# Load order and load sizes at the two ends of an attention decode step: wo in eight loads for four, w2 in four for one, K31 behind V29

## The chip, the cores and the metric

The kernel runs on one core of one Trainium2 chip. The metric is device time in microseconds (us) of one execution; the time before is 526.57 us, the median of 5 runs (525.69 to 527.09).

## The reference

A decode step for 4 sequences, one new token each, with D = 640, 32 heads of 192, a cache of 8,192 positions of which the last 2,048 are used (W = min(4096, max(256, 8192 // 4))), and a gated feed-forward of width F = 1,536. All inputs are bf16.

```python
xn  = layernorm(x)                                   # (4, 1, 640)
q   = (xn @ wq), 32 heads of 192
s   = einsum("bhqd,bhkd->bhqk", q, k_cache[:, :, -W:]) * 192 ** -0.5
o   = einsum("bhqk,bhkd->bhqd", softmax(s), v_cache[:, :, -W:])
out = x + o.reshape(4, 1, 6144) @ wo + (silu(xn @ w1) * (xn @ w3)) @ w2
```

Each head's used part of K, for all 4 sequences, is 3,072 KB, and so is its V. With wq, wo, w1, w3 and w2 the core reads 222.96 MB.

## The kernel before

*Loads.* All big loads are issued by SyncE (SP), in the order in which the program names them; SyncE waits at an issue until the buffer is free, and what stands behind it waits too. One K tile `kt` (L143) or V tile `vt` (L149) of a head is 128 rows of 24,576 B. There are 2 K buffers and 3 V buffers. At the start the three V buffers hold wq, in three transfers (L166); then come K0 and K1, and V0 as soon as the q matmuls have freed a buffer.

*Start.* x comes in through ScalarE's queue (L160), is normalised by VectorE and ScalarE (L195 to L212, result `xn`), and turned by TensorE into `xnT` (L217) and into the weights for w1, `xw`, `xh`, `xl` (L241 to L249). The rows of w1 are split: four rows on each of 128 partitions, then 64 rows as 128 half rows, and the last 64 rows as 60 and 4 "low" rows in a tile of their own, `w1e` (L409), whose unused partitions GpSimd sets to zero (L410). The low rows come in two transfers (L418: 12 rows of 15,360 B; L421: 12 rows of 1,024 B). `xm` and `xe` (L229 to L238) are copies of parts of xn laid out to match; GpSimd zeroes them first (L230, L234).

TensorE computes q on all partitions in two rounds of 30 matmuls (L263); six PSUM tiles a round are copied to `qbc`, three by VectorE and three by ScalarE in the first round, all by ScalarE in the second (L269, L271). VectorE then clears the accumulators (L277, L281), and the heads begin.

*A head.* It has four units (slots). VectorE multiplies a quarter of the K tile by q (`mult`, L298, 128x3072); TensorE adds groups of products with an identity (`adder`, L309); VectorE reduces the rest to scores (L317). A chain follows: the maximum (`lmax` L321, a transpose L326, `gmax` L331, `gneg` L334, back to all partitions L339, `negm` L342), the exponentials (L345), and `z` (L353), the exponentials laid out by sequence. TensorE multiplies z with V (`pv`, L361), ScalarE copies the result (`o_sb`, L364), and TensorE sums it over partitions into `po` (`ge_sum`, L382), with the sums of exponentials beside it (`ge_tot`, L369).

*Projection.* When a group of HG = 8 heads is in `po`, VectorE takes the reciprocal (L375), scales and transposes (`ge_turn`: og L387, oT L390), and TensorE multiplies by the group's 1,536 rows of wo and adds into `acc` (`ge_proj`, through L284). There are four groups; each takes one load of wo (128 rows of 15,360 B), save that the last one is cut into three (7, 3 and 2 twelfths of a row). There is one wo buffer, and w1e uses it first.

*Feed-forward.* w1 (L411, L412), w3 (L452) and w2 (L474) use one buffer after one another; w1's matmuls (`w1_in`, L428) run in slot 13, w3's in slot 23, and w2's (`ffn_out`, through L284) at the end.

*Order.* It is written out by hand: `add(slot, phase, fn, args)` puts each step into a table, and the steps are emitted by slot, then by phase, then in the order of the calls. K of head h is asked for at slot 4(h - 1), when the fourth multiply of head h - 2 frees its buffer, V at slot 4h + 2. At the end, K31 is asked for ahead of V29 (`early`) and goes into a V buffer; V31 goes into a K buffer. So the last loads are K30, K31, V29, V30, V31, w2 in one transfer, and the last group of wo in three. TensorE runs `ffn_out` (24 matmuls in pairs, one for each half of `acc`) and then the last `ge_proj` (24), and the result is cast by ScalarE and VectorE (L546, L547) and stored (L548).

Of the kernel before, what the change touches and what calls it, by code (L numbers as in the profile page):

```python
# [10 lines left out]
FP32 = mybir.dt.float32  # L11
# [53 lines left out]
def kernel(  # L65
# [12 lines left out]
    HG: int = 8,  # L78
    FG: int = 4,
# [23 lines left out]
    HB = HG * CT // P  # L103
    QW = HG * Dh
    RPP = QW // P
    RW = Dh // RPP
# [6 lines left out]
    assert (H * Dh) % QC == 0 and NQ % 6 == 0 and QW % P == 0 and Dh == RW * RPP and CT == HB * RW and P == FG * CT and F == FG * CT * FC  # L113
    assert 2 * H * Dh <= NJ * Dh and KBUFS == 2 and VBUFS == 3 and HB * (Dh + 1) <= 512 and H // HG > 1

# [8 lines left out]
    wopool = ctx.enter_context(tc.tile_pool(name="wo", bufs=1))  # L124
# [16 lines left out]
    def load_k(h):  # L141
        kt = (kpool if h < H - 1 else vpool).tile([P, NJ, Dh], BF16, tag="kt" if h < H - 1 else "vt", name="kt")
        nc.sync.dma_start(out=kt[:].rearrange("q j d -> q (j d)"),  # L143
                          in_=k_win[:, h].rearrange("b (p j) d -> p b (j d)", p=PB))
        kts[h] = kt

    def load_v(h):
        vt = (vpool if h < H - 1 else kpool).tile([P, NJ, Dh], BF16, tag="vt" if h < H - 1 else "kt", name="vt")
        nc.sync.dma_start(out=vt[:].rearrange("q j d -> q (j d)"),  # L149
                          in_=v_win[:, h].rearrange("b (p j) d -> p b (j d)", p=PB))  # L150
        vts[h] = vt

    def wo_load(hg, i0=0, i1=RPP):
        if i0 == 0:
            wos[hg] = wopool.tile([P, RPP * D], BF16, tag="wo", name="wo_t")
        nc.sync.dma_start(out=wos[hg][:, i0 * D:i1 * D],
                          in_=A_wo[hg * QW:(hg + 1) * QW, :].rearrange("(p i) n -> p i n", i=RPP)[:, i0:i1, :].rearrange("p i n -> p (i n)"))
# [66 lines left out]
    KM, LE, LI, LS = KC - 1, 3, 4, 5  # L224
    LP, LF = LE * LI, CT + LE * LI
    PH = D - KM * P - LP * LS - LI
    LB = KM * P + PH
    assert PH == P // 2 and F % LE == 0
    xm = ppool.tile([B, 2, PH, 2], BF16, tag="pr", name="xm")  # L229
    nc.gpsimd.memset(xm[:], 0.0)  # L230
    for i in range(2):
        nc.vector.tensor_copy(out=xm[:, i, :, i], in_=xn[:, KM * P:LB])
    xe = ppool.tile([B, LS + LE, LF], BF16, tag="pr", name="xe")
    nc.gpsimd.memset(xe[:], 0.0)  # L234
    nc.vector.tensor_copy(out=xe[:, 0:LS, CT:LF].rearrange("b s (e i) -> b s e i", i=LI),
                          in_=xn[:, LB:LB + LS * LP].rearrange("b (i e s) -> b s e i", e=LE, s=LS))
    for e in range(LE):
        nc.vector.tensor_copy(out=xe[:, LS + e, e * LI:(e + 1) * LI], in_=xn[:, LB + LS * LP:D])  # L238
    xw_ps = ps_t.tile([P, KM + 2 + LS + LE, B], BF16, tag="t", name="xw_ps")
# [4 lines left out]
    for i in range(LS + LE):  # L244
        nc.tensor.transpose(out=xw_ps[0:LF, KM + 2 + i, :], in_=xe[:, i, :], identity=idb[0:B, 0:B])

    def weights(name, p, c0, c1):
        t = const.tile([p, c1 - c0, NREP, B], BF16, name=name)
        nc.vector.tensor_copy(out=t[:], in_=xw_ps[0:p, c0:c1, :].unsqueeze(2).to_broadcast([p, c1 - c0, NREP, B]))  # L249
        return t  # L250

    xw = weights("xw", P, 0, KM)
    xh = weights("xh", P, KM, KM + 2)
    xl = weights("xl", LF, KM + 2, KM + 2 + LS + LE)
# [31 lines left out]
    def acc_add(lhsT, rhs, last=False):  # L286
        for i in range(2):
            acc_half(i, lhsT, rhs, last=last)

    po = ps_po.tile([P, HB * (Dh + 1)], FP32, name="po")  # L290
    po_v = po[:, 0:HB * Dh].rearrange("p (i x r) -> p i x r", x=HB, r=RW)
# [75 lines left out]
    def ge_tot(h):  # L367
        blk, x = (h % HG) // HB, h % HB
        nc.tensor.matmul(po[blk * CT:(blk + 1) * CT, HB * Dh + x:HB * Dh + x + 1], lhsT=tot_w[:].rearrange("p a b -> p (a b)"),  # L369
                         rhs=rsums.pop(h)[:], start=True, stop=True)  # L370
        chs.pop(h)

    def ge_rec(hg):
        rt = small.tile([P, HB], FP32, tag="rt", bufs=2, name="rt")
        nc.vector.reciprocal(out=rt[:], in_=po[:, HB * Dh:HB * (Dh + 1)])  # L375
        rts[hg] = rt

    def ge_sum(h):
        blk, x = (h % HG) // HB, h % HB
        o_sb = o_sbs.pop(h)  # L380
        for par in range(2):
            nc.tensor.matmul(po_v[blk * CT:(blk + 1) * CT, :, x, :], lhsT=sel_w[:, par].rearrange("p a b -> p (a b)"),  # L382
                             rhs=o_sb[:, par * Dh:(par + 1) * Dh].rearrange("p (r i) -> p i r", i=RPP), start=(par == 0), stop=(par == 1))

    def ge_turn(hg):
        og = small.tile([P, RPP, HB, RW], BF16, tag="og", bufs=1, name="og")
        nc.vector.tensor_tensor(out=og[:], in0=po_v, in1=rts.pop(hg)[:].unsqueeze(1).unsqueeze(3).to_broadcast([P, RPP, HB, RW]),  # L387
                                op=ALU.mult)
        oT = small.tile([P, RPP, CT], BF16, tag="oT", bufs=2, name="oT")
        nc.vector.transpose(out=oT[:].rearrange("p i r -> p (i r)"), in_=og[:].rearrange("p i x r -> p (i x r)"))  # L390
        oTs[hg] = oT

    def ge_proj(hg, i0, i1, last=False):
        oT, wo_t = oTs[hg], wos[hg]
        for i in range(i0, i1):
            acc_add(oT[:, i, 0:B], wo_t[:, i * D:(i + 1) * D], last=last and i == RPP - 1)

    FW = F // FG
# [5 lines left out]
    FM = KM * F  # L405

    def w1_load():
        wt = fpool.tile([P, FM + F // 2], BF16, tag="w", name="w1")
        we = wopool.tile([LF, LS, F], BF16, tag="wo", name="w1e")  # L409
        nc.gpsimd.memset(we[:], 0.0)  # L410
        nc.sync.dma_start(out=wt[:, 0:FM], in_=B_w1[0:KM * P, :].rearrange("(p kc) n -> p (kc n)", kc=KM))  # L411
        nc.sync.dma_start(out=wt[:, FM:], in_=B_w1[KM * P:LB, :].rearrange("r (h n) -> (r h) n", h=2))  # L412
        ffn["w1"], ffn["w1e"] = wt, we

    def w1_low(n):
        b0, we = LB + LS * LP, ffn["w1e"]
        if n == 0:
            nc.sync.dma_start(out=we[CT:LF].rearrange("p s n -> p (s n)"),  # L418
                              in_=B_w1[LB:b0, :].rearrange("(i e s) n -> e i (s n)", e=LE, s=LS))
        else:  # L420
            nc.sync.dma_start(out=we[0:LP, 0, 0:F // LE], in_=B_w1[b0:D, :].rearrange("i (e n) -> e i n", e=LE))  # L421

    def w1_in():
# [3 lines left out]
        def mm(w, lhsT, rhs, c0=0, start=False, stop=False):  # L427
            nc.tensor.matmul(ps[w * CT:(w + 1) * CT, c0:c0 + rhs.shape[1]], lhsT=lhsT.rearrange("p a b -> p (a b)"), rhs=rhs, start=start, stop=stop)  # L428

        def main(kc):  # L430
            for w in range(FG):
                mm(w, xw[:, kc], wt[:, kc * F + w * FW:kc * F + (w + 1) * FW], start=(kc == 0), stop=(kc == KM - 1))

        main(0)
        for w in range(FG):
            c0 = FM + (w % 2) * FW
            mm(w, xh[:, w // 2], wt[:, c0:c0 + FW])
        for i in range(LS):
            for w in range(FG):
                mm(w, xl[:, i], we[:, i, w * FW:(w + 1) * FW])  # L440
        FE = F // LE
        for e in range(LE):
            for w in range(FG):
                c0, c1 = max(e * FE, w * FW), min((e + 1) * FE, (w + 1) * FW)
                if c0 < c1:
                    mm(w, xl[:, LS + e], we[:, 0, c0 - e * FE:c1 - e * FE], c0 - w * FW)
# [8 lines left out]
    def w3_in():  # L455
        ffn["ps"] = ps_t.tile([P, FW], FP32, tag="t", name="f_ps")
        for kc in range(KC):
            for w in range(FG):
# [13 lines left out]
    def w2_load():  # L472
        wt = fpool.tile([P, FC, D], BF16, tag="w", name="w2")
        nc.sync.dma_start(out=wt[:].rearrange("p c n -> p (c n)"), in_=w2_v.rearrange("p c n -> p (c n)"))  # L474
        ffn["w2"] = wt

    def ffn_out():
        for c in range(FC):
            acc_add(hT[:, c, 0:B], ffn["w2"][:, c, :])
# [8 lines left out]

    ends = {H - 3: (NU - 1, NU), H - 2: (NU + 2, NU + 3), H - 1: (NU + 4, NU + 5)}
    early = {H - 1: (NU - 10, -1)}  # L490
    for h in range(H):
        u0, ul = h * GQ, h * GQ + GQ - 1
        if h >= KBUFS:
            add(*early.get(h, ((h - KBUFS + 1) * GQ, 0)), load_k, h)
# [20 lines left out]
    for hg in range(NG - 1):  # L515
        a = ((hg + 1) * HG - 1) * GQ + L + 3
        add(hg * HG * GQ + 17, 0, wo_load, hg)
        for n in range(4):
            add(a + n, 6, ge_proj, hg, n * RPP // 4, (n + 1) * RPP // 4)
    add(3, 0, w1_load)  # L520
    for n in range(2):
        add(5 + 3 * n, 1, w1_low, n)
# [9 lines left out]
    WOC = [0, RPP - 5, RPP - 2, RPP]  # L532
    for h in range(H - 2, H):
        add(NU - 6, 0, load_v, h)
    add(NU - 6, 0, w2_load)
    for i0, i1 in zip(WOC, WOC[1:]):
        add(NU - 6, 0, wo_load, NG - 1, i0, i1)
        add(e, 6, ge_proj, NG - 1, i0, i1, True)
    add(e - 1, 8, ffn_out)
# [39 lines left out]
```

## Time and profile before

| | |
|---|---|
| median of 5 runs | 526.57 us (525.69 to 527.09) |
| profiled execution: its time | 526.66 us |
| its span, first to last instruction | 524.8 us |
| granted TensorE clock, mean | 0.896 |
| TensorE, VectorE, ScalarE, GpSimd busy | 68%, 65%, 11%, 2% of the span |
| DMA queue of the loads, share of 16 engines | 99.1% |
| read from HBM | 222.96 MB, 425 GB/s over the span |

The page gives busy times, the span in 40 slices with the share of DMA time and GB/s, and groups of instructions with the idle time ahead of them and what ended it. From the trace one can ask for any stretch (busy time of each engine, clock, DMA share, GB/s), for the instructions in order of time, and for the packets of each transfer: a packet is one row of it, on one of the 16 DMA engines. A transfer has landed when the last of its engines has signalled it. An instruction's row reads: start, duration, engine, line, operation, tile written and tiles read, shapes, and in brackets the idle time ahead of it with what ended it.

### The profile page before, as it was taken

What the parts mean: (1) busy time and instruction counts of PE and PEld (TensorE: products, weight loads), DVE (VectorE), ACT (ScalarE), POOL (GpSimd) and SP (SyncE); (2) the same over time, 40 slices, a digit from 0 to 9 for tenths busy, and PEclk for the clock granted to TensorE, in tenths of its full rate; (3) what the DMA queues carried; (4) which work ended last, traced back from release to release, by engine and by line L of the source; (5) the groups of instructions that cost most, each with busy time, mean ns of one, the idle gap of its engine ahead of it and who ended that gap; (6) DMA issues with size and microseconds to landing.
All of it is one profiled execution on the core that took longest, in us unless ns stands there. A gap on an engine that the chain in (4) does not pass through costs nothing.

```text
span 524.8 us, 4807 instructions
## 1 busy us (share of the span) xinstructions
PE 357.5 (68%) x2347; PEld 76.1 (14%) x1652; DVE 340.2 (65%) x397; ACT 57.3 (11%) x179; POOL 8.2 (2%) x11
## 2 busy tenths in 40 slices
PE   0777877674668776683867776664776776675786
PEld 0100121111111111110111111111111121111122
DVE  3349776385666777673667867663776767666951
ACT  2030122000101110110110111100011110011010
POOL 4200000000000000000000000000000000000000
PEclk9988898876887998888797989988798898889998
DMA  9999999999999999999999999999999999999996
GB/s 388 425 442 393 434 430 422 432 436 433 435 428 435 430 429 432 433 433 433 430 433 428 431 434 433 428 435 431 435 427 439 425 431 438 427 436 427 438 423 267
DMA packets 11155, 223.27 MB, mean 425 GB/s; under 512 B 1246, under 2 KB 1394, under 8 KB 1650
## 3 DMA queue, kind: packets, MB, share of 16 engines
q1 hardware_dynamic: 11118, 222.96, 99.1%
q8 instruction: 16, 0.26, 0.2%
q14 instruction: 5, 0.04, 0.0%
q10 hardware_dynamic: 16, 0.01, 0.0%
HBM read 222.96 MB, written 0.01 MB: 425 GB/s over the span
## 4 chain that ended last, share of the span: by engine, by line
DMA 60%; DVE 19%; PE 16%; ACT 2%; issue 2%; SPq 0%; DVEq 0%
DMA kt<-in_A_k_cache_dram 52%; DVE pr L298 13%; PE ps L309 8%; DMA w<-in_B_w_dram 6%; PE po L382 3%; DVE sc L317 3%; PE qps L263 2%; DVE z L353 1%; DMA x_sb<-in_A_x_dram 1%; ACT ex L345 1%; PE acc L284 1%; DVE xn L212 1%; PE mt L339 1%; ACT L345 0%; PE f_ps L428 0%
## 5 line engine op out<-in xcount | busy, mean ns | idle before, releaser
L309 PE MATMUL ps<-pr,idb 128*128 128x512 bf16 x768 | 211.3, 416 | 142.5 <-DVE pr L298 142.5
L298 DVE TENSOR_TENSOR pr<-kt,qbc 128x3072 bf16<-128x3072 bf16 x128 | 223.5, 1747 | 100.9 <-DMA kt<-in_A_k_cache_dram 100.9
L317 DVE TENSOR_REDUCE sc<-ps 128x16 f32<-128x512 f32 x128 | 87.1, 681 | 2.4 <-PE ps L309 2.4
L361 PE MATMUL o_ps<-vt,z 128*8 128x384 bf16 x1024 | 56.0, 363 | 1.8 <-DMA vt<-in_A_v_cache_dram 1.8
L382 PE MATMUL po<-o_sb,sel_w 128*32 128x192 f32 x128 | 48.5, 513 | 1.1 <-ACT o_sb L364 1.1
L361 PEld LDWEIGHTS <-z 128*8 128x8 bf16 x1024 | 25.0, 92 | 100.7 <-issue 90.9
L353 DVE TENSOR_TENSOR z<-ex,mask_b 128x256 bf16<-128x256 bf16 x32 | 13.6, 425 | 36.1 <-ACT ex L345 36.0
L364 ACT COPY o_sb<-o_ps 128x384 f32<-128x384 f32 x32 | 15.3, 478 | 188.8 <-PE o_ps L361 188.8
L334 ACT ACTIVATE gneg<-gmax 1x128 f32<-1x128 f32 x32 | 9.8, 308 | 169.2 <-DVE gmax L331 169.2
L326 PEld LDWEIGHTS mt<-idf,lmax 128*1 128x1 f32 x32 | 3.3, 103 | 135.2 <-issue 133.2
L382 PEld LDWEIGHTS po<-o_sb,sel_w 128*32 128x32 f32 x128 | 14.1, 130 | 27.8 <-issue 24.4
L309 PEld LDWEIGHTS <-idb 128*128 128x128 bf16 x123 | 11.9, 97 | 37.5 <-issue 31.2
L339 PEld LDWEIGHTS mt<-ones_ff,gneg 1*128 1x128 f32 x64 | 9.4, 182 | 47.3 <-issue 40.0
L263 PE MATMUL qps<-wt,xnT 128*128 128x512 bf16 x60 | 15.7, 426 | 0.0
L331 DVE TENSOR_REDUCE gmax<-mt 1x4 f32<-1x128 f32 x32 | 8.8, 275 | 6.6 <-PE mt L326 6.6
L342 ACT COPY negm<-mt 128x1 f32<-128x1 f32 x32 | 5.1, 159 | 70.3 <-PE mt L339 70.3
L339 PE MATMUL mt<-ones_ff,gneg 1*128 1x1 f32 x64 | 12.1, 256 | 0.7 <-ACT gneg L334 0.7
L369 PEld LDWEIGHTS po<-rsum,tot_w 128*32 128x32 f32 x64 | 4.5, 108 | 49.1 <-ACT ex L345 35.0
L217 PE MATMUL xnT_ps<-idb,xn 4*128 4x4 bf16 x5 | 0.4, 178 | 16.3 <-DVE xn L212 16.3
L345 ACT ACTIVATE ex<-sc,negm 128x64 bf16<-128x64 f32 x32 | 11.1, 348 | 1.0
L326 PE MATMUL mt<-idf,lmax 128*1 128x128 f32 x32 | 10.8, 337 | 0.0
L284 PE MATMUL acc<-wo_t,oT 128*4 128x320 bf16 x96 | 9.9, 327 | 0.0
(74 smaller groups left out, 81.1 us busy)
## 6 DMA issues: line engine op xcount, KB each, us to landing
kt<-in_A_k_cache_dram SPq DMA_DIRECT2D x32, 3072.0 KB, 18.6
vt<-in_A_v_cache_dram SPq DMA_DIRECT2D x32, 3072.0 KB, 25.0
wt<-in_A_wq_dram SPq DMA_DIRECT2D x2, 3072.0 KB, 9.8
wo_t<-in_A_wo_dram SPq DMA_DIRECT2D x3, 1920.0 KB, 23.3
w<-in_B_w_dram SPq DMA_DIRECT2D x2, 1920.0 KB, 26.9
wt<-in_A_wq_dram SPq DMA_DIRECT2D x1, 1536.0 KB, 19.6
w<-in_B_w_dram SPq DMA_DIRECT2D x1, 1536.0 KB, 15.9
wo_t<-in_A_wo_dram SPq DMA_DIRECT2D x1, 1120.0 KB
```

What stands on the lines that cost most here:

```text
L263: nc.tensor.matmul(qp[:], lhsT=xnT[:, kc].rearrange("p a b -> p (a b)"), rhs=wq_rows[kc][:, (c0 + i) * QC:(c0 + i + 1) * QC], start=(kc == ...
L284: nc.tensor.matmul(acc[i * CT:i * CT + B, :], lhsT=lhsT, rhs=rhs[:, i * N0:(i + 1) * N0], start=first, stop=last)
L298: nc.vector.tensor_tensor(out=pr[:], in0=kts[h][:, g * JQ:(g + 1) * JQ, :], in1=qbc[:, h * Dh:(h + 1) * Dh].unsqueeze(1).to_broadcast([P, ...
L309: nc.tensor.matmul(ps[:], lhsT=idb[:], rhs=pr[:, :, kk * DD:(kk + 1) * DD], start=(kk == 0), stop=(kk == NK - 1))
L317: nc.vector.tensor_reduce(out=scs[h][:, g * JQ:(g + 1) * JQ], in_=pss.pop(u)[:], axis=AX.X, op=ALU.add)
L326: nc.tensor.transpose(out=mt[0:1, 0:P], in_=chs[h][0][:], identity=idf[:])
L339: nc.tensor.matmul(mt[:, P:P + 1], lhsT=gneg[:].rearrange("o p b -> o (p b)"), rhs=ones_ff[:], start=True, stop=True)
L345: nc.scalar.activation(out=ex[:], in_=scs.pop(h)[:], func=ACTF.Exp, bias=negm[:, 0:1], scale=SCALE, accum_out=rsum[:])
L353: nc.vector.tensor_tensor(out=z[:], in0=ex[:].unsqueeze(2).to_broadcast([P, NJ, B]), in1=mask_b[:].unsqueeze(1).to_broadcast([P, NJ, B]), ...
L361: nc.tensor.matmul(o_ps[c * CT:c * CT + 2 * B, :], lhsT=z[:, 2 * jj:2 * jj + 2, :], rhs=vt[:, 2 * jj:2 * jj + 2, :], start=(jj < 4), stop= ...
L364: nc.scalar.copy(out=o_sb[:], in_=o_ps[:])
L382: nc.tensor.matmul(po_v[blk * CT:(blk + 1) * CT, :, x, :], lhsT=sel_w[:, par].rearrange("p a b -> p (a b)"), rhs=o_sb[:, par * Dh:(par + 1 ...
```

## The change

Five things differ; the functions are those of the listing.

1. HG is 4: eight groups of heads, each with its own reciprocal, scaling, transpose and load of wo (128 rows of 7,680 B), in two wo buffers. Group hg's load is asked for at slot 16 hg + 8; the last two groups' at the end.
2. w2 comes in four transfers (4, 4, 3 and 1 twelfths), and TensorE takes them one by one.
3. K31 is asked for in its turn, behind V29, and uses a K buffer; V31 a V buffer.
4. The order at the end is V30, V31, w2 first and second, wo seventh and eighth, w2 third and fourth, and the matmuls follow it.
5. The low rows of w1 come in four transfers of 12 rows (6,144, 6,144, 3,072 and 1,024 B), the first two into w1e, the others into the tail of w1's own tile. GpSimd clears 44x3072 of w1e and 44x1536 of w1's tail in place of 44x7680. The copies into xe are six for four, the transposes for w1 twelve for fourteen.

```diff
-    HG: int = 8,
-    FG: int = 4,
+    HG: int = 4,
...
-    wopool = ctx.enter_context(tc.tile_pool(name="wo", bufs=1))
+    wopool = ctx.enter_context(tc.tile_pool(name="wo", bufs=2))
...
     def load_k(h):
-        kt = (kpool if h < H - 1 else vpool).tile([P, NJ, Dh], BF16, tag="kt" if h < H - 1 else "vt", name="kt")
+        kt = kpool.tile([P, NJ, Dh], BF16, tag="kt")
...
-    def wo_load(hg, i0=0, i1=RPP):
-        if i0 == 0:
-            wos[hg] = wopool.tile([P, RPP * D], BF16, tag="wo", name="wo_t")
-        nc.sync.dma_start(out=wos[hg][:, i0 * D:i1 * D],
-                          in_=A_wo[hg * QW:(hg + 1) * QW, :].rearrange("(p i) n -> p i n", i=RPP)[:, i0:i1, :].rearrange("p i n -> p (i n)"))
+    def wo_load(hg):
+        wo_t = wopool.tile([P, RPP * D], BF16, tag="wo")
+        nc.sync.dma_start(out=wo_t[:], in_=A_wo[hg * QW:(hg + 1) * QW, :].rearrange("(p i) n -> p (i n)", i=RPP))
+        wos[hg] = wo_t
...
-    nc.vector.tensor_copy(out=xe[:, 0:LS, CT:LF].rearrange("b s (e i) -> b s e i", i=LI),
-                          in_=xn[:, LB:LB + LS * LP].rearrange("b (i e s) -> b s e i", e=LE, s=LS))
+    for g in range(2):
+        b0 = LB + g * 2 * LP
+        nc.vector.tensor_copy(out=xe[:, 0:2, g * CT:g * CT + LP].rearrange("b s (e i) -> b s e i", i=LI),
+                              in_=xn[:, b0:b0 + 2 * LP].rearrange("b (i e s) -> b s e i", e=LE, s=2))
+    nc.vector.tensor_copy(out=xe[:, 2, 0:LP].rearrange("b (e i) -> b e i", i=LI),
+                          in_=xn[:, LB + 4 * LP:LB + 5 * LP].rearrange("b (i e) -> b e i", e=LE))
...
     def w1_load():
-        wt = fpool.tile([P, FM + F // 2], BF16, tag="w", name="w1")
-        we = wopool.tile([LF, LS, F], BF16, tag="wo", name="w1e")
+        w = B_w1
+        wt = fpool.tile([P, FH + F], BF16, tag="w", name="w1")
+        we = wopool.tile([LF, 2 * F], BF16, tag="wo", name="w1e")
         nc.gpsimd.memset(we[:], 0.0)
+        nc.gpsimd.memset(wt[0:LF, FH:], 0.0)
...
     def w1_low(n):
-        b0, we = LB + LS * LP, ffn["w1e"]
-        if n == 0:
-            nc.sync.dma_start(out=we[CT:LF].rearrange("p s n -> p (s n)"),
-                              in_=B_w1[LB:b0, :].rearrange("(i e s) n -> e i (s n)", e=LE, s=LS))
+        w, wt, we = B_w1, ffn["w1"], ffn["w1e"]
+        if n < 2:
+            b0 = LB + n * 2 * LP
+            nc.sync.dma_start(out=we[n * CT:n * CT + LP, :],
+                              in_=w[b0:b0 + 2 * LP, :].rearrange("(i e s) n -> e i (s n)", e=LE, s=2))
+        elif n == 2:
+            nc.sync.dma_start(out=wt[0:LP, FH:FH + F], in_=w[LB + 4 * LP:LB + 5 * LP, :].rearrange("(i e) n -> e i n", e=LE))
         else:
-            nc.sync.dma_start(out=we[0:LP, 0, 0:F // LE], in_=B_w1[b0:D, :].rearrange("i (e n) -> e i n", e=LE))
+            nc.sync.dma_start(out=wt[CT:LF, FH:FH + F // LE], in_=w[LB + 5 * LP:D, :].rearrange("i (e n) -> e i n", e=LE))
...
-    def w2_load():
-        wt = fpool.tile([P, FC, D], BF16, tag="w", name="w2")
-        nc.sync.dma_start(out=wt[:].rearrange("p c n -> p (c n)"), in_=w2_v.rearrange("p c n -> p (c n)"))
-        ffn["w2"] = wt
+    W2C = [0, FC - 8, FC - 4, FC - 1, FC]
+
+    def w2_load(i):
+        if i == 0:
+            ffn["w2"] = fpool.tile([P, FC, D], BF16, tag="w", name="w2")
+        c0, c1 = W2C[i:i + 2]
+        nc.sync.dma_start(out=ffn["w2"][:, c0:c1, :].rearrange("p c n -> p (c n)"),
+                          in_=w2_v[:, c0:c1, :].rearrange("p c n -> p (c n)"))
...
-    ends = {H - 3: (NU - 1, NU), H - 2: (NU + 2, NU + 3), H - 1: (NU + 4, NU + 5)}
-    early = {H - 1: (NU - 10, -1)}
+    ends = {H - 2: (NU - 1, NU), H - 1: (NU + 3, NU + 4)}
...
-            add(*early.get(h, ((h - KBUFS + 1) * GQ, 0)), load_k, h)
+            add((h - KBUFS + 1) * GQ, 0, load_k, h)
...
-    for hg in range(NG - 1):
+    for hg in range(NG - 2):
         a = ((hg + 1) * HG - 1) * GQ + L + 3
-        add(hg * HG * GQ + 17, 0, wo_load, hg)
-        for n in range(4):
-            add(a + n, 6, ge_proj, hg, n * RPP // 4, (n + 1) * RPP // 4)
+        add(hg * HG * GQ + 8, 0, wo_load, hg)
+        add(a, 6, ge_proj, hg, 0, RPP // 2)
+        add(a + 1, 6, ge_proj, hg, RPP // 2, RPP)
     add(3, 0, w1_load)
-    for n in range(2):
-        add(5 + 3 * n, 1, w1_low, n)
+    for n in range(4):
+        add(4 + 2 * n, 1, w1_low, n)
...
-    add(NU - 6, 0, w2_load)
-    for i0, i1 in zip(WOC, WOC[1:]):
-        add(NU - 6, 0, wo_load, NG - 1, i0, i1)
-        add(e, 6, ge_proj, NG - 1, i0, i1, True)
-    add(e - 1, 8, ffn_out)
+    add(NU - 6, 0, w2_load, 0)
+    add(NU - 6, 0, w2_load, 1)
+    add(NU - 6, 0, wo_load, NG - 2)
+    add(NU - 6, 0, wo_load, NG - 1)
+    add(NU - 6, 0, w2_load, 2)
+    add(NU - 6, 0, w2_load, 3)
+    add(e - 1, 8, ffn_out, 0)
+    add(e - 1, 8, ffn_out, 1)
+    add(e - 1, 8, ge_proj, NG - 2, 0, RPP)
+    add(e, 6, ge_proj, NG - 1, 0, RPP)
+    add(e, 7, ffn_out, 2)
+    add(e, 7, ffn_out, 3)
```

## The prediction

> **What bounds the kernel.** I read the 40 slices first: they show which resource never rests.
>
> ```profile
> DMA  9999999999999999999999999999999999999996
> GB/s 388 425 442 393 434 430 422 432 436 433 435 428 435 430 429 432 433 433 433 430 433 428 431 434 433 428 435 431 435 427 439 425 431 438 427 436 427 438 423 267
> DMA packets 11155, 223.27 MB, mean 425 GB/s; under 512 B 1246, under 2 KB 1394, under 8 KB 1650
> ```
>
> The DMA engines are busy in every slice but the last; TensorE and VectorE stand at 68% and 65% of the span. The groups say the same: the multiplies (L298) waited 100.9 us for K tiles. So three things set the time: what delays the DMA stream at its start or opens a hole in it, what the bytes cost in transfer time, and what runs after the last byte. Work of an engine inside the stream costs nothing until it makes a load late. A busy 9 covers 90 to 100%, so I asked for stages. The fourth slice (39 to 52 us, 393 GB/s) is low, and holds the hole:
>
> ```profile
> 30.00:44.00 14.00, 10.41 (x35) 0.30 (x3) 8.21 (x9) 3.03 (x6) 0.00 (x0) 0.76 1.00 432
> 44.00:54.00 10.00, 6.63 (x31) 0.80 (x8) 8.62 (x11) 2.19 (x5) 0.00 (x0) 1.00 0.96 396
> ```
>
> The last two columns are DMA share and GB/s. From 44 to 54 us the share is 0.96: 0.4 us of all 16 engines is lost. The trace's packet records are finer: between 46.2 and 47.2 us each engine pauses for 0.36 to 0.88 us, 0.58 us on average, and from then to 517 us no engine pauses. The cause stands in the loads' queue:
>
> ```profile
> 30.97 0.43 SPq L412 DMA_DIRECT2D w<-in_B_w_dram  x1
> 44.92 0.54 SPq L143 DMA_DIRECT2D kt<-in_A_k_cache_dram  x1
> ```
>
> SyncE issued the rest of w1 at 30.97 us, and the third K tile only at 44.92, because that K buffer came free when head 0's four multiplies ended. By 46.2 the loads ahead of it had drained; its packets began at 46.34 to 47.17 us. Why were the multiplies so late? The start:
>
> ```profile
> 8.45 0.54 DVE L201 TENSOR_SCALAR xc<-xf,negmean 4x640 f32<-4x640 f32 x1
> ...
> 9.05 0.38 POOL L234 MEMSET xe<- 4x352 bf16 x1 [6.94 <-DVE xc L201]
> 9.38 6.49 POOL L410 MEMSET w1e<- 44x7680 bf16 x1
> ...
> 11.58 4.63 DVE L212 TENSOR_SCALAR xn<-xc,rstd 4x640 bf16<-4x640 f32 x1
> ```
>
> The same kind of VectorE operation on 4x640 takes 0.54 us at L201 and 4.63 at L212, and the long one ends at 16.21 us, 0.34 after GpSimd's memset of w1e ends at 15.87: it stood still while the memset ran. Everything of the start (transposes, the q matmuls from 17.93, the first multiply at 35.40) follows from xn.
>
> **The change, part by part.**
>
> *Start.* The memsets shrink. Their rate from L234 and L410 is (6.49 - 0.38)/(7680 - 352) = 0.83 ns a column, so w1e with 3,072 columns takes 2.65 us and the new memset of w1's last 1,536 columns 1.37: they end near 12.0 and 13.4 us in place of 15.87. xn then ends near 12.3 (if VectorE gets in between the two) or 13.7 in place of 16.21: 2.5 to 3.9 us sooner. Against that stand two more xe copies (0.15 to 0.20 us each by L238 and L235), while two of the 0.06 us transposes (L245) go: 2.2 to 3.6 us sooner at the q matmuls. These don't meet a later DMA: the last part of wq lands at 20.7 us, and its matmuls, which began at 25.3, would begin at 21.7 or later. So the third K is issued at 41.3 to 42.7 us, well before the 44.0 that 46.2 allows (2.25 us from issue to its slowest first packet). The hole closes: -0.6 us; bounds 0 (xn isn't freed) and -0.9 (the longest pause).
>
> *More packets.* A packet is one row of a transfer. The packet records give 912 ns for 24,576 B, 573 for 15,360, 338 for 8,960, 149 for 3,840, 102 for 2,560, 46 for 1,024, and on an engine each starts 4 ns before the end of the one ahead. The split wo of before shows what a cut costs: 338 + 149 + 102 - 573 - 2x4 = 8 ns for two cuts, 4 ns each. After, wo has 1,024 packets for 768, w2 512 for 128: 640 more, 40 an engine, 40 x 4 = 0.16 us. Seven more transfers (86 for 79) each add one 9 ns semaphore packet an engine, 0.04 us. The four small w1 transfers have 48 packets for 24, on three engines: 0.04. Sum +0.25 us, all of it on the stream; bounds +0.15 and +0.5 (8 ns a cut with no overlap).
>
> A rule of the skill speaks against the change here: DMA: Bandwidth & Descriptors, "Anatomy of one DMA", has a fixed cost of about 2.0 us a transfer, which for seven more would make 14 us, an estimate by that page. The row against it: wo's three pieces landed at 519.65, 520.78 and 521.57 us, 1.13 and 0.79 apart, what their packets take (8x145 and 8x98 ns) and no more; behind one another in a full queue nothing of 2 us shows.
>
> *Queue order.* K31 goes from before to behind V29, so it lands at 497.9 us in place of 490.6 (a 3 MB tile takes 7.27); wo's first group is asked for 28 us sooner, in front of V2. The last of w1's rows come behind V2, near 80 us, where the w1 matmuls (L428) started at 74.96; they and the reductions behind them on TensorE start some 5 us later, and the fifth K would be issued near 86 us in place of 84.57. V3 and w3 are queued until about 97 us then: cover of 10 us, so nothing. Were it gone, the cost would be those 1.4 us. V30 no longer waits for head 28's sums. Eight rounds of og, oT and the reciprocal on half the width, in place of four at 0.54 + 0.58 + 0.16 us, add some 1.3 us to VectorE, hidden in its 100.9 us of waiting for K.
>
> *The tail.* Here is the end of before:
>
> ```profile
> 508.27 0.42 DVE L353 TENSOR_TENSOR z<-ex,mask_b 128x256 bf16<-128x256 bf16 x1 [1.48 <-ACT ex L345]
> ...
> 512.42 1.47 PE L361 MATMUL o_ps<-vt,z 128*8 128x384 bf16 x32 [1.36 <-DMA vt<-in_A_v_cache_dram]
> ...
> 517.02 2.77 PE L284 MATMUL acc<-w,hT 128*4 128x320 bf16 x24 [1.04 <-DMA w<-in_B_w_dram]
> ...
> 519.69 2.46 PE L284 MATMUL acc<-wo_t,oT 128*4 128x320 bf16 x24
> ...
> 522.19 0.48 DVE L547 CAST res<-acc 4x320 bf16<-4x320 f32 x1 [5.00 <-PE acc L284]
> ```
>
> V31 lands at 512.38, w2 at 516.98, wo in three pieces to 521.57; the cast follows 0.62 us after that, since TensorE still worked off earlier pieces at half clock. After: the multiplies of head 31 start at 497.9; from K30's landing to the end of its fourth multiply took 483.31 to 493.22, 9.9 us, and from there to z 5.3 (503.4 to 508.7), so z comes at 513.1, 0.7 us after V31 in place of 3.7 before it. The last sums end near 516.7. The first two w2 pieces (in by 515.5) then take 8 pairs of 0.135 us, to 517.8; wo's seventh group lands at 517.8, its eighth at 520.1, the two last w2 pieces at 521.2 and 521.6: TensorE waits for each and is free 1.4 us before the eighth. Behind the last byte stand one pair of matmuls, 0.04 + 0.30 us, in place of two and a backlog: 0.37 to the cast, -0.25. But TensorE now waits between pieces, and if the clock is at half for the last 8 to 10 pairs, each takes 0.27, some +0.3 at the cast. I take -0.1.
>
> Will the clock fall there? In the windows of before it is 0.50 from 518 to 521 us, although TensorE had rested for 1.0 us only (516.0 to 517.02) since head 31's sums. The Trainium skill (TensorE: Matmul & The Clock Gate, "Part 1: The HAM clock gate") has it halve after an idle window of some 3.4 us; by that rule the tail of after, whose waits are at most 1.9 us, would keep the full clock and the term would be -0.25, an estimate by that page. The row shows half clock after shorter rests, so the middle value stands.
>
> *Sum.* -0.6 + 0.25 - 0.1 = -0.45 us on the profiled execution (526.66 us, 1.86 around its span of 524.8): 526.2. The median of the five runs is 526.57, 0.09 lower: **526.1 us**.
>
> **Rivals.**
>
> *TensorE late behind K31 (slower).* Place: from pv of head 31 to the last pair. With a half clock from 512.7 to 521.1, pv takes 2.9 us, the sums 3.0, the 8 pairs 2.1, and the 16 pairs behind start at 521.3, past the last landing: the cast comes at 523.8 in place of 522.19, +1.6, 528.1 us; with half a clock only from 514.3, 523.0 and 527.4. It decides from about 3 us of half clock there, where the slack of 1.4 us is gone. For it: the mean granted clock is 0.896, and z loses 3 us of lead. Against: half-clock stretches are mostly 3.4 us long, and w2's first pieces were done sooner.
>
> *The latest engines get lighter (faster).* At the end the queues run dry one by one:
>
> ```profile
> 518.00:519.00 1.00, 1.00 (x10) 0.52 (x8) 0.00 (x0) 0.00 (x0) 0.00 (x0) 0.50 0.77 321
> 519.00:520.00 1.00, 1.00 (x10) 0.44 (x8) 0.00 (x0) 0.00 (x0) 0.00 (x0) 0.50 0.69 279
> 520.00:521.00 1.00, 1.00 (x12) 0.46 (x10) 0.00 (x0) 0.00 (x0) 0.00 (x0) 0.50 0.59 221
> ```
>
> The first engine ended 3.34 us before the last. w1's 12 rows of 15,360 B went to three engines, four each (2.3 us); before them the landings of one transfer spread over 0.7 us, after them over 2.4. If the four transfers of the change fall on different engines, those three end up to 1.8 us sooner and the next, 0.6 to 1.0 behind, decide: -0.9, 525.2 us. Against: the second w1e transfer (12 rows of 1,024 B) ran on the three latest engines too.
>
> *The start isn't freed.* If xn still waits for the memsets, or the q matmuls start as late, the hole stays: 526.7 us.
>
> **How the numbers follow.** Forecast 526.1 us, chance 0.52, own range 525.6 to 526.8; the hole stays, 526.7, 0.10; faster rival 525.2, 0.18; slower rival 527.4 to 528.1, 0.20. A measurement of this kernel tells about 0.2% (1.05 us, 525.5 to 527.6) from no change: faster 0.18, same 0.62, slower 0.20. The range runs from the faster rival's 525.2 to 527.8, inside the slower one's.
>
> **What would show it.** After should have xn done by 14 us, the third K issued before 43, a DMA share of 0.99 or more from 44 to 54 us, transfers to 521 us that land one after another, z of head 31 near 513, and the cast within 0.5 us of the last landing. A low share in another stage, or a cast a microsecond behind the last landing, would make the prediction wrong.

## The result, and the profile after

After: 525.59 us, the median of 24 runs (525.38 to 525.92). Before, beside them: 526.63 us, the median of 42 (525.48 to 527.75). The ratio is 0.9981, 95% interval 0.9975 to 0.9986. The profiled execution of after took 525.42 us; its span is 523.5 us, its mean clock 0.902.

The 40 slices of after, as read for before:

```profile
DMA  9999999999999999999999999999999999999996
GB/s 389 424 438 423 439 433 423 432 438 428 431 430 436 428 427 441 426 434 432 430 430 437 428 437 426 436 428 438 426 430 434 433 430 435 428 434 431 434 424 280
DMA packets 11904, 223.26 MB, mean 426 GB/s; under 512 B 1332, under 2 KB 1608, under 8 KB 3052
```

The fourth slice moved 423 GB/s where before moved 393: the hole is gone. The same two stages show it more sharply (the last two columns are DMA share and GB/s):

```profile
30.00:44.00 14.00, 8.78 (x27) 0.10 (x1) 11.29 (x12) 2.53 (x6) 0.00 (x0) 0.76 1.00 429
44.00:54.00 10.00, 5.79 (x26) 0.80 (x8) 8.31 (x11) 2.19 (x5) 0.00 (x0) 0.96 1.02 432
```

432 GB/s stand against 396, and the packet records hold no pause on any engine. In the loads' queue the third K tile is issued 3.1 us sooner than before:

```profile
27.89 0.43 SPq L408 DMA_DIRECT2D w<-in_B_w_dram  x1
41.84 0.54 SPq L140 DMA_DIRECT2D kt<-in_A_k_cache_dram  x1
```

The instructions of the start, in order of time, tell why:

```profile
9.28 2.65 POOL L405 MEMSET w1e<- 44x3072 bf16 x1
...
11.55 2.04 DVE L209 TENSOR_SCALAR xn<-xc,rstd 4x640 bf16<-4x640 f32 x1
11.88 1.37 POOL L406 MEMSET w<- 44x1536 bf16 x1
...
15.35 3.17 PE L258 MATMUL qps<-wt,xnT 128*128 128x512 bf16 x7
```

The two memsets took the 2.65 and 1.37 us that were worked out. xn still stood still beside them, and VectorE did not get in between the two, but the second ended at 13.25, so that xn was done at 13.59 in place of 16.21 and the q matmuls began at 15.35 in place of 17.93.

The tail, in order of time:

```profile
511.81 0.43 DVE L347 TENSOR_TENSOR z<-ex,mask_b 128x256 bf16<-128x256 bf16 x1 [1.47 <-ACT ex L339]
...
514.36 0.57 PE L279 MATMUL acc<-w,hT 128*4 128x320 bf16 x6
...
516.87 0.98 PE L279 MATMUL acc<-wo_t,oT 128*4 128x320 bf16 x12 [0.97 <-DMA wo_t<-in_A_wo_dram]
...
519.14 0.98 PE L279 MATMUL acc<-wo_t,oT 128*4 128x320 bf16 x12 [1.29 <-DMA wo_t<-in_A_wo_dram]
...
520.30 0.71 PE L279 MATMUL acc<-w,hT 128*4 128x320 bf16 x8 [0.18 <-DMA w<-in_B_w_dram]
...
521.05 0.48 DVE L557 CAST res<-acc 4x320 bf16<-4x320 f32 x1 [4.28 <-PE acc L279]
```

TensorE waits for each piece and is idle 1.29 us before wo's eighth group. The 16 matmuls of w2's first two pieces ran from 514.36 between the passes of the f32 sums. The last landing is at 520.67 (before 521.57), and the cast follows after 0.37 us (before 0.62). The clock stood at full:

```profile
518.00:519.00 1.00, 0.00 (x0) 0.00 (x0) 0.00 (x0) 0.00 (x0) 0.00 (x0) 1.00 0.72 294
519.00:520.00 1.00, 0.86 (x12) 0.53 (x12) 0.00 (x0) 0.00 (x0) 0.00 (x0) 1.00 0.63 248
520.00:521.00 1.00, 0.81 (x10) 0.34 (x7) 0.00 (x0) 0.00 (x0) 0.00 (x0) 1.00 0.10 37
```

**Where the time went.** The cast moved from 522.19 to 521.05, by 1.14 us. The last load lands engine by engine; averaged over the 16 engines (below: the mean landing) that is 0.76 us earlier, 520.43 to 519.67. The last engine's lag behind that mean is 0.14 smaller (1.14 to 1.00), and the piece from there to the cast 0.24 smaller. The packet records, added up, say when the gain arose: the first 18 MB had come at 43.78 us in both, 20 MB at 49.51 before and 48.75 after, 40 MB at 95.96 and 94.96, 219 MB at 511.15 and 510.30. All of it arises by 40 MB; what follows gives a little back.

### The profile page after: what moved, and what is told of

It is laid out like the page before. It is cut to its first block, busy times and chain, and to the rows that moved or that the text cites. A ratio compares the mean times of both kernels' runs of the same rounds, so it can differ in the third digit from the quotient of the medians.

```text
span 523.5 us, 4813 instructions
## 1 busy us (share of the span) xinstructions
PE 356.0 (68%) x2337; PEld 74.5 (14%) x1643; DVE 339.4 (65%) x410; ACT 57.3 (11%) x179; POOL 5.6 (1%) x12
## 4 chain that ended last, share of the span: by engine, by line
DMA 60%; PE 20%; DVE 15%; ACT 3%; issue 2%; SPq 0%; DVEq 0%
DMA kt<-in_A_k_cache_dram 44%; PE ps L303 12%; DMA w<-in_B_w_dram 10%; DVE pr L292 10%; DMA vt<-in_A_v_cache_dram 5%; PE po L376 4%; DVE sc L311 2%; PE qps L258 1%; ACT ex L339 1%; DVE z L347 1%; DMA x_sb<-in_A_x_dram 1%; PE mt L333 1%; PE o_ps L355 1%; ACT L339 0%; ACT negm L336 0%
## 5 line engine op out<-in xcount | busy, mean ns | idle before, releaser
L303 PEld LDWEIGHTS <-idb 128*128 128x128 bf16 x124 | 11.9, 96 | 38.5 <-issue 32.3
L333 PEld LDWEIGHTS mt<-ones_ff,gneg 1*128 1x128 f32 x64 | 9.4, 182 | 46.1 <-issue 42.7
```

Of the source, the lines that this page charges most:

```text
L303: nc.tensor.matmul(ps[:], lhsT=idb[:], rhs=pr[:, :, kk * DD:(kk + 1) * DD], start=(kk == 0), stop=(kk == NK - 1))
L333: nc.tensor.matmul(mt[:, P:P + 1], lhsT=gneg[:].rearrange("o p b -> o (p b)"), rhs=ones_ff[:], start=True, stop=True)
```

## The experiments

Each ratio is to before, run beside the experiment, with its 95% interval in brackets.

**1. e1_late_memset**: before, with only its memset of w1e put off until the start is over. GpSimd first copies one element of `xl`.

```diff
         we = wopool.tile([LF, LS, F], BF16, tag="wo", name="w1e")
+        nc.gpsimd.tensor_copy(out=late[:], in_=xl[0:1, 0, 0, 0:1])
         nc.gpsimd.memset(we[:], 0.0)
```

> The kernel before, with the memset of w1e held back until xl is written (GpSimd first copies one element of xl). Theory A (the memset holds xn back, so the third K is issued late and the DMA stream has a hole, 0.6 us of pause and 0.3 us of slow first packets): xn ends near 12 us, the third K is issued near 41, no pause between 44 and 54 us, 0.9 us faster than before (525.7). Theory B (the gain of the change comes from the order and cut of the last loads alone): same as before, 526.6, whatever the start does.

Measured: 525.57 us, ratio 0.9984 (0.9975 to 0.9993). The start of its profile:

```profile
11.66 0.54 DVE L212 TENSOR_SCALAR xn<-xc,rstd 4x640 bf16<-4x640 f32 x1
...
14.71 6.49 POOL L412 MEMSET w1e<- 44x7680 bf16 x1
...
38.74 0.55 SPq L143 DMA_DIRECT2D kt<-in_A_k_cache_dram  x1
```

and the stage of the hole:

```profile
44.00:54.00 10.00, 6.88 (x53) 1.57 (x38) 5.24 (x6) 1.91 (x5) 0.00 (x0) 0.86 1.02 433
```

With no memset beside it xn takes 0.54 us in place of 4.63. The third K is issued at 38.74, nothing pauses, and the mean landing is 519.47, 0.96 sooner than before's. One late memset is worth the whole change (525.57 against 525.59): the memset's hold on xn, not the new loads, makes the gain, and the other parts of the change together add nothing that can be told.

**2. e2_long_memset**: after, with w1e cleared twice.

```diff
         nc.gpsimd.memset(we[:], 0.0)
+        nc.gpsimd.memset(we[:], 0.0)
         nc.gpsimd.memset(wt[0:LF, FH:], 0.0)
```

> The changed kernel, with w1e cleared twice, so that GpSimd is busy until some 16.2 us as in the kernel before. Theory A: xn ends near 16.4, the third K is issued near 45 us, the pause at 46 to 47 us is back, 0.9 us slower than the changed kernel (526.5). Theory B: as the changed kernel, 525.6. If VectorE gets in between two memsets, xn ends at 13.6 or sooner and nothing changes.

Measured: 527.09 us, 1.0010 (0.9997 to 1.0022), 1.5 us over after. Its start:

```profile
11.38 0.72 DVE L209 TENSOR_SCALAR xn<-xc,rstd 4x640 bf16<-4x640 f32 x1
11.81 2.89 POOL L406 MEMSET w1e<- 44x3072 bf16 x1
...
12.95 1.83 DVE L227 COPY xm<-xn 4x64 bf16<-4x64 bf16 x2
13.15 1.66 DVE L232 COPY xe<-xn 4x24 bf16<-4x24 bf16 x2
...
14.80 1.36 DVE L237 COPY xe<-xn 4x4 bf16<-4x4 bf16 x3
...
43.20 0.54 SPq L140 DMA_DIRECT2D kt<-in_A_k_cache_dram  x1
```

and the stage of the hole:

```profile
44.00:54.00 10.00, 5.61 (x27) 0.80 (x8) 8.62 (x10) 2.19 (x5) 0.00 (x0) 1.00 0.99 401
```

Here xn did get in between two memsets, but the small copies behind it stood still (the pair into `xm` takes 1.83 us, in e1 0.29). The third K came at 43.20; engines paused until 47.2, 0.41 to 0.45 us on average, and the first packets after the pause were slow, 0.48 us more. The mean landing is 0.94 us later than after's, which is the expected price. The loss was larger because the engines also ended less evenly: the last landing is 1.8 us behind the mean, in after 1.0.

The Trainium skill (SBUF — State Buffer, "SBUF: two separate sides") says that GpSimd and VectorE's wider modes share a port pair as an exclusive lock, held by the one that starts first for its whole instruction. 0.54 us alone against 2.04 and 4.63 beside a memset agree with it for xn; in which mode xn ran, no row says.

**3. e3_k31_in_turn**: before, with after's place and buffer for K31 and V31 (items 3 and 4 of the change, without its pieces).

```diff
-    ends = {H - 3: (NU - 1, NU), H - 2: (NU + 2, NU + 3), H - 1: (NU + 4, NU + 5)}
-    early = {H - 1: (NU - 10, -1)}
+    ends = {H - 2: (NU - 1, NU), H - 1: (NU + 3, NU + 4)}
+    early = {}
```

> The kernel before with one part of the change alone: K31 in its turn behind V29 and in a K buffer, V31 in a V buffer. Theory A: z of head 31 comes some 4.5 us later, near 513, still ahead of w2's landing at 517; 526.6, within 0.2 us of before. Rival (TensorE is late behind K31): its last sums end after w2 has landed, the cast moves with them, 0.5 to 1.5 us slower.

Measured: 526.74 us, 1.0005 (0.9996 to 1.0014). No gain and no cost of K31's place shows; the interval reaches from 0.2 us faster to 0.7 slower, and experiment 6 is the sharper test.

**4. e4_w2_last**: before, with w2 cut into eleven and one twelfths, the one behind wo.

```diff
+    W2C = [0, FC - 1, FC]
...
+    add(NU - 6, 0, w2_load, 1)
+    add(e - 1, 8, ffn_out, 0)
+    add(e, 7, ffn_out, 1)
```

> The kernel before with the tail's cut alone: w2 in two transfers, 11 twelfths in its old place and the last twelfth behind wo's third piece, and one pair of matmuls behind it. Theory A: the start is as before, the hole stays; the cast follows the last landing by 0.4 us in place of 0.6, so 0.1 to 0.25 us faster than before (526.45). Theory B: it holds most of the gain of the change, 525.7.

Measured: 526.62 us, 1.0006 (0.9994 to 1.0017). The cast follows the last landing by 0.38 us, so the profile shows the piece, but a scatter of 2 to 3 us, before's and its own, hides it in the median: inconclusive on the time.

**5. e5_late_memset_w2_last**: the edits of 1 and 4 together.

> The first experiment (kernel before, memset held back, no hole: 525.57) and the tail's cut of the fourth together. With the hole gone the runs spread by 0.6 us only, so a tail of 0.4 us behind the last landing in place of 0.6 to 0.9 should show: 525.3. If the tail is worth nothing, 525.6.

Measured: 525.60 us, 0.9988 (0.9978 to 0.9997). Against experiment 1, both at full clock around the last landing, the cast is 0.38 us after it in place of 0.51: a short last piece is worth 0.13 us there. Four of the 11 times lie between 526.1 and 527.2; why is not known, and the medians don't show the 0.13.

**6. e6_late_k31_in_turn**: the edits of 1 and 3 together.

> The first experiment with K31 in its turn behind V29, z of head 31 some 4.5 us later. Without the hole its own price shows: 525.6 if TensorE's slack of more than 1 us covers it; 526.1 to 527 if TensorE is late behind K31.

Measured: 525.61 us, 0.9984 (0.9974 to 0.9993). The profiled execution (525.97) had half clock from 513.2 to 520.0:

```profile
518.00:519.00 1.00, 1.00 (x10) 0.49 (x8) 0.00 (x0) 0.00 (x0) 0.00 (x0) 0.50 0.75 305
519.00:520.00 1.00, 1.00 (x10) 0.53 (x8) 0.00 (x0) 0.00 (x0) 0.00 (x0) 0.50 0.65 239
```

There the cast comes 0.81 us after the last landing, 0.3 more than in experiment 1. With K31 late and the clock at half, both together, TensorE is late, and that costs tenths, not 1.6 us; the median shows no cost.

**7. e7_after_late_memset**: after, with its memsets put off as in 1.

> The changed kernel with both memsets held back until xl is written. xn ends 1.7 us sooner still, the third K is issued near 40 us. Theory A: the changed kernel has no hole any more, so a start that is sooner still gives nothing: 525.6, as the changed kernel. If the start counts beyond the hole, 1 us or more faster.

Measured: 525.50 us, 0.9977 (0.9969 to 0.9986). Once the pause is gone, an earlier start gives nothing that can be told. It is the best version tried, within after's scatter.

**8. e8_v_halves**: after, with 30 V tiles in two transfers each; 30 more loads.

```diff
-            add(u0 + 2, 0, load_v, h)
+            add(u0 + 2, 0, load_v, h, 2)
```

> The changed kernel with V of heads 0 to 29 in two transfers each, rows of 12,288 B for 24,576: 30 more transfers and 3,840 more packets. By the packet records, 4 ns a packet and 6 ns a transfer on each engine: 30 x (8 x 4 + 6) ns = 1.1 us slower than the changed kernel (526.7). If a transfer has a fixed cost of 2 us in the stream, 60 us slower. If cuts are free behind one another, 525.6.

Measured: 527.72 us, 1.0025 (1.0015 to 1.0034), 2.13 over after. The mean landing is 1.96 us later than after's. 0.67 us of it is lost by 20 MB, in the cut V0 (from 35 to 38.5 us the engines pause for 0.16 us on average, and packets of 12,288 B take up to 698 ns for 460). The other 29 cut loads lose 1.29 us, 45 ns each for 128 more packets, 8 an engine: about 6 ns a packet, the semaphore packet included.

**9. e9_v1_ahead**: before, with V1 asked for ahead of the third K, so that 3 MB more are queued while that K waits.

```diff
-            add(u0 + 2, 0, load_v, h)
+            add(*((4, -1) if h == 1 else (u0 + 2, 0)), load_v, h)
```

> The kernel before, its long memset and its late third K left as they are, but V1 asked for ahead of the third K (its buffer is free from some 30 us on), so that the stream has 7 us more to do while the third K waits. Theory A (the hole in the stream is the price, not the late start itself): no pause at 46 to 47 us, 525.6, although xn still ends at 16.2 us. If the late start counts in another way, 526.6.

Measured: 527.57 us, 1.0013 (1.0003 to 1.0023): this expectation fell. Two stages of it:

```profile
44.00:54.00 10.00, 6.56 (x30) 0.80 (x8) 8.62 (x11) 2.19 (x5) 0.00 (x0) 1.00 1.03 440
70.00:80.00 10.00, 8.11 (x57) 1.65 (x42) 7.70 (x9) 1.08 (x4) 0.00 (x0) 0.83 0.98 391
```

The hole at 46 us is gone, and a new one stands at 74.9 to 77.2 (0.40 us an engine on average): the third K landed 7.1 us later, so the loads that wait for its multiplies were issued late, the last one below at 73.77 for before's 68.79:

```profile
32.28 0.55 SPq L149 DMA_DIRECT2D vt<-in_A_v_cache_dram  x1
44.86 0.53 SPq L143 DMA_DIRECT2D kt<-in_A_k_cache_dram  x1
...
73.77 0.54 SPq L143 DMA_DIRECT2D kt<-in_A_k_cache_dram  x1
```

Reordering moved the pause; only the earlier start removed it.

**10. e10_low_more**: after, with two more 12-row transfers of 6,144 B rows into unused partitions of w1e (which is made 128 partitions high for 44), read by nothing.

```diff
+    def low_more(n):
+        nc.sync.dma_start(out=ffn["w1e"][64 + n * CT:64 + n * CT + LP, :],
+                          in_=B_w1[LB:LB + 2 * LP, :].rearrange("(i e s) n -> e i (s n)", e=LE, s=2))
...
+    for n in range(2):
+        add(10, 2, low_more, n)
```

> The changed kernel with two more transfers of 12 rows of 6,144 B that nothing reads, after w1's low rows, into unused partitions of w1e: four packets more on each of three engines, 2 x 4 x 230 ns = 1.84 us there and nothing on the other 13. If these three engines are among the last at the end: 1.7 to 1.9 us slower (527.4). If a lighter engine takes them: 525.6.

Measured: 529.03 us, 1.0041 (1.0026 to 1.0055), 3.44 over after, more than any theory gave. The mean landing is 2.11 us later than after's, and three engines end last (0, 0.75 and 0.76 us ahead of the end, the next 1.68). These are probably the three that take the low rows, slowed by the added ones; how near the end they stood without them isn't shown. Most of the 2.11 us was lost from 80 to 85 us; first this kernel, then after:

```profile
80.00:85.00 5.00, 4.54 (x32) 1.08 (x26) 0.00 (x0) 0.62 (x2) 0.00 (x0) 0.61 1.02 295
```

```profile
80.00:85.00 5.00, 4.79 (x32) 1.08 (x26) 0.00 (x0) 0.66 (x3) 0.00 (x0) 0.60 1.04 446
```

The share is full and the rate is not: packets of 24,576 B took up to 1,940 ns for 912. The slow packets lie beside the 24 added ones, which ran from 79.8 to 83.3 us and took 484 ns in the median, where the packets of w1's own two transfers of this size (at 53 and 61 us) took 234 and slowed nothing. So the added transfers bring it; whether by the partitions that they write or by rows that are read again, nothing here separates, and the cause stays open.

**11 and 12. e11_w1_on_8, e12_w1_on_16**: experiment 4, with w1's last 128 rows as plain rows in one transfer, grouped by 8 or by 16, and without xm, xe and the memset.

```diff
+    NE = 8
...
-        we = wopool.tile([LF, LS, F], BF16, tag="wo", name="w1e")
-        nc.gpsimd.memset(we[:], 0.0)
...
+        nc.sync.dma_start(out=wt[:, FM:], in_=B_w1[KM * P:D, :].rearrange("(e i) n -> e i n", e=NE))
```

> The kernel of the fourth experiment (before, last twelfth of w2 at the end) with w1's last 128 rows in one plain transfer, written as 8 groups of 16 rows, in place of the half rows and the low rows; no w1e, no memset of it, fewer transposes and matmuls. No hole: 525.5 from that. If the transfer runs on 8 engines (1.9 us each) that are the light ones of the end: 0.3 to 0.6 us less, 525.0. If they are the heavy ones: 1 us or more slower, 526.5.

> As the experiment with 8 groups, with 16 groups of 8 rows: 0.94 us on each of 16 engines, no engine is singled out. No hole: 525.5 from that; against the three engines of before and after, the last engines of the end get 0.4 us more or 2 us less, according to which are last: 525.5 to 525.9.

Measured: 525.77 us, 0.9981 (0.9971 to 0.9991), and 525.72 us, 0.9982 (0.9972 to 0.9991). Both have no pause, mean landings at 519.47 and 519.49, and the last at 521.04 and 521.01. The two behave alike, so the grouping didn't single out eight engines, and the test of that is inconclusive. What they do show: without low rows the last landing lies 0.6 us later than in experiment 5 (520.45) at the same mean (519.51). So the low rows seem to lie on engines that would else end early.

## Why the prediction was right, step by step

Forecast 526.1, measured 525.59: inside the range, and a hair below the forecast's own 525.6 to 526.8. The mechanism held, but the gain, 1.04 us, is over twice the 0.45 that was added up, and it is in part luck that the range held it: its lower end was drawn for another rival. On the profiled executions the sum is −0.96 (start) + 0.20 (packets) − 0.14 (the last engine's lag, which had no term) − 0.24 (tail) = −1.14 us, for −0.6 + 0.25 − 0.1. The start's term was too small, and the tail's.

*Start, −0.6: right in mechanism, mis-sized.* xn was done at 13.59 (12.3 or 13.7 predicted, the second being the case without a gap), the third K issued at 41.84 (41.3 to 42.7). Experiment 1 prices it: −0.96 us in mean landing, just past the bound of −0.9. The step counted the pause (0.58 us mean) and not the slow restart: before's 29 packets of 24,576 B begun from 46.2 to 48.3 us took up to 1,631 ns in place of 912, which is 0.32 us an engine. 0.58 + 0.32 = 0.90. Busy time hides this: the DMA share of 0.96 showed 0.4 us, while the GB/s column beside it (396 against 432 over 10 us, 0.83 us of transfer time) held nearly all. That column stood in the prediction and was not used. Its latest safe issue of the third K, 44.0 us, was too late as well: in experiment 2 an issue at 43.20 still left a pause.

*Packets, +0.25: right.* After against experiment 1, both without a pause: mean landing +0.20, last landing +0.25 (one profiled execution each, and the order differs too). The Trainium skill's 2.0 us a transfer (DMA: Bandwidth & Descriptors, "Anatomy of one DMA") is stated there for GpSimd's queue, which the prediction did not say; these loads are SyncE's, and experiment 8 measures 45 ns for a cut load in a full queue.

*Queue order, nothing: right in sum, wrong in one number.* K31 landed at 496.9 (497.9 predicted, less the hole). But the K predicted near 86 us came 3.5 later (it is the sixth K issued, not the fifth as the prediction has it):

```profile
80.21 0.83 PE L427 MATMUL f_ps<-w,xl 44*32 44x384 bf16 x10 [4.61 <-DMA w<-in_B_w_dram]
...
86.76 0.42 DVE L347 TENSOR_TENSOR z<-ex,mask_b 128x256 bf16<-128x256 bf16 x1 [10.04 <-ACT ex L339]
...
89.48 0.55 SPq L140 DMA_DIRECT2D kt<-in_A_k_cache_dram  x1
```

The low rows landed near 80 as reckoned, but behind w1's matmuls stood a head's whole chain on TensorE, and behind z the multiplies on VectorE: 10 us of waiting. The loads ahead of that K are 41.1 MB by their sizes, which at after's 94.96 us for 40 MB and 432 GB/s last until about 97.5: 8 us of cover, so nothing was lost.

*Tail, −0.1: the full-clock value came.* It was −0.24. Other runs split it: with before's order the cast comes 0.51 us after the last landing in experiments 3 and 9, at full clock all through the tail, and in 1, at full clock from 518.8 us on. So the half clock made 0.11 of before's 0.62, and the order 0.14. The middle value was drawn from before's half clock after a rest of 1.0 us; after rested 1.29 us and kept full clock to 524.3. What decides between them isn't settled here. z of head 31 came at 511.81, 1.3 sooner than reckoned, 0.9 of that by the hole.

*The rivals.* TensorE late: in none of the profiles by 1.6 us; at most 0.3 to 0.4 (experiment 6). The slack was larger than the 1.4 us reckoned (0.97 us idle before wo's seventh group and 1.29 before its eighth), because w2's first matmuls cost no time of their own between the f32 passes. Its price was also set too high: 527.4 to 528.1 add the delay to before's time and leave out the −0.6 and +0.25 of the same sum; with them it is some 527.0 to 527.8. The latest engines getting lighter: the measured 525.59 is nearer to its 525.2 than to the forecast, but for another reason. The lag fell by only 0.14 of the 0.9 it asked for, experiment 1 has the gain with before's low rows, and experiments 11 and 12, without low rows, end less evenly, not more. A time that fits a rival is no proof of it. The start not freed: refuted by xn's row.

*The scatter.* Kernels whose profile has a pause vary by 2 us and more (before, 2, 3, 4; 9 by 1.7), those without mostly by 0.3 to 0.7 (after, 1, 7, 11, 12). That a pause hits the engines unevenly from run to run fits, but is only argued; 5, 6 and 8 don't sort so cleanly. Before is not slower every time: 5 of its 42 times lie from 525.48 to 525.69, in after's range, and the next at 526.06. What those executions did otherwise no trace here shows; the gain of 1 us is that of the median.

## What to carry to other kernels

In a kernel bound by its loads, look for the stage where the stream pauses and follow back what issued that load late; here a memset on one engine froze a 0.5 us operation on another, 30 us earlier. Price a pause by the GB/s of its stage, not by the DMA share, and check that a reordering doesn't move the pause to where the moved load is missed. More and smaller transfers in a full queue cost tens of nanoseconds each; the order of the last pieces is worth tenths of a microsecond.

## What the runs showed of the hardware

- A stream that restarts is slow at first: packets of 24,576 B took up to 1,631 ns for 912 after the pause of before (0.32 us an engine) and up to 2,418 in experiment 2 (0.48 us), and up to 1,802 ns at the very start.
- The lead that a load needs is not told by its first packets elsewhere: before's third K had its first packets 1.4 to 2.25 us after the issue, yet in experiment 2, issued at 43.20 with the queue running dry about 46, seven engines paused. Issued at 41.84 nothing paused.
- Whether VectorE gets in between two memsets in a row varies: in experiment 2 it did, in after not.
- 24 added packets to unused partitions slowed all engines for some 3.5 us (295 GB/s at a full share from 80 to 85 us, experiment 10); unexplained.
